# Seven groups of an MLP product on column tiles of TensorE's array

## The chip, the core and the metric

The kernel runs on one core of a Trainium2 chip. Its time is the device time of one execution in microseconds (us); the time before is the median of three runs. A profile is one further execution, taken with the hardware profiler.

## What is computed

One transformer block on a sequence of S = 2048 rows with D = 1024: layer normalization, attention of 32 heads in a sliding window of 256, a residual sum, a second layer normalization, an MLP with F = 3584 and a residual sum. Inputs and output are bfloat16. The reference, cut:

```python
x = A_x
h = x + _A_ref(_layernorm(x, axis=-1), A_wqkv, A_wo)
h2 = h + _B_ref(_layernorm(h, axis=-1), B_w1, B_w2)

def _B_ref(x, w1, w2):
    h = jnp.einsum("bsd,df->bsf", x, w1)
    h = _silu(h)
    out = jnp.einsum("bsf,fd->bsd", h, w2)
    return out
```

The change lies in the first product of the last function, `x @ w1`.

## The kernel before

The sequence is cut into NB = 4 blocks of 512 rows. The kernel first computes queries, keys, values and the attention of the blocks, with the scores of one block laid between the matmuls of the next block's projections (lines 240 and 250) by a hand-written stream; `wo_group` (line 271) multiplies by `wo`. Then comes the MLP, block by block: all of the first product of a block, then all of its second.

The first product of a block has FT = 28 column groups of 128 columns of `w1`. `h1_group(b, ft)` (line 666) computes one group: it takes one PSUM bank of [128 x 512] from a rotation of six (`next_acc`; the banks are called acc and hacc in the profile) and sums KT = 8 matmuls in it (line 669). Each of them has a [128 x 128] piece of `w1` as the stationary operand, the weights, and 512 columns of `ln2T[b]`, the transposed normalized rows, as the moving operand. TensorE loads weights with an instruction of its own (LDWEIGHTS, "PEld" in the profile) and then streams the moving operand past them. A "step" below is one of the eight values of `kt`.

```python
acc = next_acc()
for kt in range(KT):
    nc.tensor.matmul(acc, lhsT=w1[:, kt, ft * P:(ft + 1) * P], rhs=ln2T[b][:, kt, :],
                     start=(kt == 0), stop=(kt == KT - 1))
```

After each group `silu` (line 676) has ScalarE compute a tanh from the bank (line 678) and VectorE combine it with the bank into `gT` (line 679), which is the stationary operand of the second product, `mm2` (line 706). In the last block (b = 3) nothing else runs beside this loop: its 28 groups follow one another, and `mm2` follows them.

The order on every engine is the order in which the code issues instructions (`tc.manual_schedule()`); no planner moves them.

A matmul can also take a part of the array, a tile: rows of the array by columns. Its place is given by `tile_position=(row, column)`, and its output goes to the PSUM partitions of its columns. The kernel does this already in the attention's scores: `scores_xy` (matmul in line 303) and `scores_0` (line 355) run on tiles of 32 rows by 64 columns, eight of them for the four heads of a group and two halves of the keys, and `scores_c` (line 329) on tiles of 32 rows by 128 columns. Line 383 is the product of attention weights and values, on the whole array with 33 moving columns.

Of the kernel before, what the change touches and what calls it, by code (L numbers as in the profile page):

```python
# [14 lines left out]
P = 128  # L15
# [22 lines left out]
    [(0, "X", 2), (1, "Y", 1), (2, "X", 3)],  # L38
    [(1, "Y", 2), (2, "C", 1), (3, "Y", 3)],
]  # L40
SPLIT = [(0, 8), (8, 16), (16, 21), (21, 27), (27, 32)]


@with_exitstack
def kernel(
# [10 lines left out]
    nc = tc.nc  # L56
# [8 lines left out]
    KT = D // P  # L65
# [29 lines left out]
    def view(region, off, *dims):  # L95
        n = 1
        for d in dims:
            n *= d
        ap = region[:, off:off + n]
        if len(dims) == 2:  # L100
            return ap.rearrange("p (a b) -> p a b", b=dims[1])
        if len(dims) == 3:
            return ap.rearrange("p (a b c) -> p a b c", b=dims[1], c=dims[2])
        return ap
# [3 lines left out]
    w1 = view(r_w, 0, KT, F)  # L108
# [17 lines left out]
    ln2T = [view(r_a, w2_off + 4096 * 5, KT, 512), view(r_e, 0, KT, 512), view(r_e, 4096, KT, 512), view(r_e, 0, KT, 512)]  # L126
# [104 lines left out]
    def next_acc():  # L231
        acc_n[0] += 1
        return acc_banks[acc_n[0] % len(acc_banks)]
# [54 lines left out]
    def scores_xy(b, g, odd):  # L288
        q0 = odd * P
        mid, first, last = odd, odd - 2, odd + 2  # L290

        parts = [
            (mid, 0, q0, q0 + 320, 64), (mid, 1, q0 + 64, q0 + 384, 128),
            (last, 0, q0 + 256, q0 + 384, 384), (first, 1, q0, q0 + 128, 0),
            (first, 0, q0, q0 + 64, 0), (last, 1, q0 + 320, q0 + 384, 448),
        ]
        for step in range(3):
            for hh in range(4):
                for kt, half, qa, qb, col in parts[step * 2:step * 2 + 2]:
                    r0 = hh * DH  # L300
                    t = b * 4 + kt
                    k0 = (t % 4) * P + half * 64
                    nc.tensor.matmul(  # L303
                        sc[hh // 2][half * 64:half * 64 + 64, hh % 2, col:col + qb - qa],
                        lhsT=kT[t // 4][r0:r0 + DH, g, k0:k0 + 64],
                        rhs=qT[b][r0:r0 + DH, g, qa:qb],
                        start=True, stop=True, tile_position=(r0, half * 64),
                    )
        for pair in range(2):
            e = xy_ring[((b * G + g) % 2 * 2 + odd) * 2 + pair]  # L310
            tri = e[:, 0:1024].rearrange("p (h c q) -> p h c q", h=2, q=256)
            bank = sc[pair]
            both = bank[:, :, 0:192]
            both = bass.AP(tensor=both.tensor, offset=both.offset, ap=[*both.ap[:2], [320, 2], both.ap[2]])
            nc.scalar.activation(out=tri[:, :, :, 64:256], in_=both, func=ACT.Exp, scale=scale)  # L315
            nc.scalar.activation(out=e[:, 1024:1280].rearrange("p (h q) -> p h q", q=P), in_=bank[:, :, 192:320], func=ACT.Exp, scale=scale)  # L316
            four = e[:, 0:1024].rearrange("p (c q) -> p c q", q=256)
            select(four[:, :, 0:P], four[:, :, 64:64 + P], False)
            select(four[:, :, P:2 * P], four[:, :, P:2 * P], True)
# [86 lines left out]
    def attn_piece(b, g, first, last):  # L406

        for k in range(2):
            a, z = max(first - 16 * k, 0), min(last - 16 * k, 16)
            if a < z:  # L410
                attn_out(b, g + k, a, z)
                if z == 16:
                    late.append(lambda k=k: attn_transpose(b, g + k))

    class Stream:
# [3 lines left out]
        def __init__(self, b):  # L419
# [4 lines left out]
            for g in range(0, G, 2):  # L424
                if b:
                    self.bursts += [lambda g=g: scores_c(b, g)]
                    self.bursts += [lambda g=g, k=k, o=o: scores_xy(b, g + k, o) for k in range(2) for o in range(2)]
                    self.pieces += [lambda g=g, s=s: attn_piece(b, g, *s) for s in SPLIT]
                else:
# [235 lines left out]

    def h1_group(b, ft):
        acc = next_acc()
        for kt in range(KT):
            nc.tensor.matmul(acc, lhsT=w1[:, kt, ft * P:(ft + 1) * P], rhs=ln2T[b][:, kt, :],  # L669
                             start=(kt == 0), stop=(kt == KT - 1))  # L670
        return acc

    th_first = [r_e[:, 1024 * i:1024 * (i + 1)].bitcast(F32) for i in range(2)]
# [9 lines left out]
    for b in range(NB):  # L683
# [4 lines left out]
        for ft in range(FT):  # L688
            acc = h1_group(b, ft)
            run_late()  # L690
            if extra:
                extra.pop(0)[0]()
            if b == 0 and ft == 4:
                for i in (1, 2, 3, 4):
                    load_w2(i)
            silu(b, acc, ft)
            if b == 0 and 7 <= ft < 15:
                j, c = divmod(ft - 7, 2)
                wo_group(NB - 1, j, c)
# [59 lines left out]
```

## Time and profile before

| | |
|---|---|
| median of three runs | 691.17 us (691.05 to 691.21) |
| the profiled execution, first to last instruction (span) | 688.9 us (688.92) |
| the profiled execution's own time outside its span | not given by the page; the median of the runs is 2.25 us above the span |
| TensorE busy | 685.2 us (99%), 6011 matmuls and as many weight loads |
| VectorE, ScalarE, GpSimd busy | 291.2, 244.2, 160.8 us |
| granted TensorE clock, mean | 1.000 |
| one matmul of line 669 | 128x512, 379 ns from start to modelled end |
| first product of the last block | 589.3 to 637.6 us of the span |

Busy time of a matmul runs from its start to its modelled end, and matmuls overlap: the 379 ns are how long one is under way, not the distance to the next one. That distance is read from the starts. In a merged timeline row, the first number is the start of the first instruction, the second the time until the last one's end, and the xN how many instructions the row merges; a row carries the shape of its first instruction. In the view by windows, a column "0.03 (x8)" is the busy time in the window and the number of instructions that were under way in it; after TensorE's matmuls (PE) and weight loads (PEld) come the granted clock, the share of DMA and GB/s.

### The profile page before, as it was taken

How to read it: one execution, taken by the hardware profiler on the slowest of the kernel's cores; microseconds unless marked ns; L12 is line 12 of the kernel's file. 1: busy time of each engine (PE TensorE's matmuls, PEld its weight loads, DVE VectorE, ACT ScalarE, POOL GpSimd, SP SyncE). 2: the span in 40 equal slices, each digit the busy share in tenths (PEclk: the TensorE clock that was granted, in tenths of full speed). 3: DMA queues.
4: the chain of work that ended last, by engine and by line, in shares of the span. 5: the costliest groups of instructions: out<-in, count | busy, mean ns of one | idle time of the engine just before them, and what ended most of it. 6: DMA issues, size and time to landing. Idle time of an engine off the chain costs nothing.

```text
span 688.9 us, 14243 instructions
## 1 busy us (share of the span) xinstructions
PE 685.2 (99%) x6011; PEld 342.3 (50%) x6011; DVE 291.2 (42%) x613; ACT 244.2 (35%) x464; POOL 160.8 (23%) x295
## 2 busy tenths in 40 slices
PE   9999999999999999999999999999999999999998
PEld 4445555555555555544444444444444444444445
DVE  5267647744444449444316133342233251333111
ACT  7326666666667666421300033300133100233000
POOL 1006666566666656400000000000000000000000
PEclk9999999999999999999999999999999999999999
DMA  7832231126241889871023310022300123100110
GB/s 259 275 64 69 40 85 57 25 63 186 71 131 21 257 252 272 199 267 40 23 88 112 84 39 0 1 91 70 85 0 1 21 96 90 39 1 1 30 39 24
DMA packets 78641, 61.48 MB, mean 89 GB/s; under 512 B 52465, under 2 KB 62705, under 8 KB 78577
## 3 DMA queue, kind: packets, MB, share of 16 engines
q1 hardware_dynamic: 77888, 59.78, 30.2%
q8 instruction: 47, 0.77, 0.4%
q10 hardware_dynamic: 688, 0.79, 0.3%
q14 instruction: 18, 0.14, 0.1%
HBM read 39.85 MB, written 8.39 MB: 70 GB/s over the span
## 4 chain that ended last, share of the span: by engine, by line
PE 99%; DVE 0%; issue 0%
PE hacc L669 19%; PE hacc L706 18%; PE acc L250 17%; PE acc L706 11%; PE acc L669 9%; PE acc L240 7%; PE acc L271 7%; PE o_ps L383 5%; PE sc L303 3%; PE hacc L271 2%; PE sc L355 1%; PE o_ps L240 1%; PE o_ps L167 1%; PE sc L329 1%; PE acc L525 0%; PE o_ps L525 0%
## 5 line engine op out<-in xcount | busy, mean ns | idle before, releaser
L373 POOL TENSOR_SCALAR_AFFINE_SELECT r_e<-r_e 128x512 bf16<-128x512 bf16 (+1 forms) x288 | 157.8, 563 | 123.9 <-ACT r_e L363 60.8
L706 PEld LDWEIGHTS <-r_a 128*128 128x128 bf16 x952 | 90.9, 98 | 103.0
L669 PEld LDWEIGHTS <-r_w 128*128 128x128 bf16 x896 | 87.3, 98 | 104.8
L706 PE MATMUL hacc<-r_a 128*128 128x512 bf16 (+2 forms) x616 | 122.5, 360 | 0.0
L669 PE MATMUL hacc<-r_e,r_w 128*128 128x512 bf16 x456 | 100.9, 379 | 0.0
L315 ACT ACTIVATE r_e<-sc 128x768 bf16<-128x768 f32 x96 | 78.2, 814 | 47.9 <-PE sc L303 47.9
L678 ACT ACTIVATE r_n<-hacc 128x512 f32<-128x512 f32 x30 | 17.9, 597 | 178.9 <-PE hacc L669 178.9
L250 PEld LDWEIGHTS <-r_w 128*128 128x128 bf16 x512 | 47.1, 98 | 55.0 <-issue 1.0
L706 PE MATMUL acc<-r_a 128*128 128x512 bf16 x336 | 74.0, 379 | 0.0
L252 DVE CAST r_a<-acc 128x512 bf16<-128x512 f32 x56 | 38.7, 692 | 57.7 <-PE acc L250 57.4
L250 PE MATMUL acc<-r_t,r_w 128*128 128x512 bf16 x256 | 59.6, 380 | 0.0
L250 PE MATMUL acc<-r_w 128*128 128x512 bf16 x256 | 57.8, 380 | 0.0
L383 PEld LDWEIGHTS <-r_e 128*128 128x128 bf16 x1440 | 47.4, 96 | 17.9
L669 PE MATMUL acc<-r_e,r_w 128*128 128x512 bf16 x216 | 49.1, 379 | 0.0
L271 PE MATMUL acc<-r_o,r_a 128*128 128x512 bf16 x208 | 48.7, 380 | 0.0
L383 PE MATMUL o_ps<-r_a,r_e 128*128 128x33 bf16 x1440 | 48.1, 178 | 0.0
L721 DVE SCALAR_TENSOR_TENSOR r_t<-hacc,r_t 128x512 bf16<-128x512 f32 (+2 forms) x22 | 14.0, 635 | 56.7 <-PE hacc L706 56.7
L316 ACT ACTIVATE r_e<-sc 128x256 bf16<-128x256 f32 x96 | 37.6, 392 | 0.0
L271 PEld LDWEIGHTS <-r_a 128*128 128x128 bf16 x256 | 23.4, 98 | 26.9
L721 DVE SCALAR_TENSOR_TENSOR r_t<-acc,r_t 128x512 bf16<-128x512 f32 x12 | 8.3, 692 | 64.2 <-PE acc L706 64.2
L679 DVE SCALAR_TENSOR_TENSOR r_a<-r_n,hacc 128x512 bf16<-128x512 f32 x30 | 20.6, 687 | 33.0 <-ACT r_n L678 33.0
L669 PE MATMUL hacc<-r_a,r_w 128*128 128x512 bf16 x144 | 33.0, 379 | 0.0
(100 smaller groups left out, 539.6 us busy)
## 6 DMA issues: line engine op xcount, KB each, us to landing
r_w<-in_B_w_dram SPq DMA_DIRECT2D x8, 896.0 KB, 5.2
r_a<-in_B_w_dram SPq DMA_DIRECT2D x7, 1024.0 KB, 7.5
r_w<-in_A_wqkv_dram SPq DMA_DIRECT2D x4, 1024.0 KB, 7.8
h_dram<-r_t SPq DMA_DIRECT2D x16, 256.0 KB, 3.1
r_t<-h_dram SPq DMA_DIRECT2D x16, 256.0 KB, 2.8
out_dram<-r_t SPq DMA_DIRECT2D x31, 128.0 KB, 1.7
r_o<-in_A_x_dram SPq DMA_DIRECT2D x15, 256.0 KB, 4.6
r_e<-h_dram SPq DMA_DIRECT2D x3, 1024.0 KB, 5.7
```

Source lines behind the costliest of these rows:

```text
L240: nc.tensor.matmul(acc, lhsT=lnT_b[b % 2][:, kt, j * P:(j + 1) * P], rhs=wv[:, kt, c * 512:(c + 1) * 512], start=(kt == 0), stop=(kt == KT ...
L250: nc.tensor.matmul(acc, lhsT=wqk[:, kt, col0:col0 + P], rhs=lnT_b[b % 2][:, kt, :], start=(kt == 0), stop=(kt == KT - 1))
L252: copy(out=(qT, kT)[which][b][:, g, :], in_=acc)
L271: nc.tensor.matmul(acc, lhsT=qT[b][:, g, j * P:(j + 1) * P], rhs=wo[:, g, c * 512:(c + 1) * 512], start=(g == 0), stop=(g == G - 1))
L303: nc.tensor.matmul(sc[hh // 2][half * 64:half * 64 + 64, hh % 2, col:col + qb - qa], lhsT=kT[t // 4][r0:r0 + DH, g, k0:k0 + 64], rhs=qT[b] ...
L315: nc.scalar.activation(out=tri[:, :, :, 64:256], in_=both, func=ACT.Exp, scale=scale)
L316: nc.scalar.activation(out=e[:, 1024:1280].rearrange("p (h q) -> p h q", q=P), in_=bank[:, :, 192:320], func=ACT.Exp, scale=scale)
L373: nc.gpsimd.affine_select(out=dst, in_=src, pattern=[[0, n] for n in dst.shape[1:-1]] + [[sgn, P]], compare_op=ALU.is_ge if upper else ALU ...
L383: nc.tensor.matmul(o_ps[pair][:, qt * 2 + hh, 0:VW], lhsT=chunk_of(i, bank, piece, pair, hh), rhs=v[:, b * 4 + kt, g * 4 + pair * 2 + hh, ...
L669: nc.tensor.matmul(acc, lhsT=w1[:, kt, ft * P:(ft + 1) * P], rhs=ln2T[b][:, kt, :], start=(kt == 0), stop=(kt == KT - 1))
L706: nc.tensor.matmul(acc[:, 0:c1 - c0], lhsT=gT[:, ft, j * P:(j + 1) * P], rhs=w2[ft // 4][:, ft % 4, c0:c1], start=(ft == 0), stop=(ft == F ...
L721: nc.vector.scalar_tensor_tensor(out=t_out[j % 2][:, c0:c1], in0=acc[:, 0:c1 - c0], scalar=0.5, in1=t_in[j % 2][:, c0:c1], op0=ALU.mult, o ...
```

## The change

A table names seven groups of the last block and the width of their column tiles, 64 or 32. For these, every matmul of a step is replaced by two or four, each over all 128 rows of the array and 64 or 32 of its columns, with that part of the weights and the whole moving operand of 512 columns; each writes its own part of the bank's partitions. The tiles of one step come one after another in the code, before the next step. All other groups are as before.

```diff
     [(0, "X", 2), (1, "Y", 1), (2, "X", 3)],
     [(1, "Y", 2), (2, "C", 1), (3, "Y", 3)],
 ]
+COLS = {(3, 8): 64, (3, 9): 64, (3, 12): 32, (3, 13): 32, (3, 16): 64, (3, 17): 32, (3, 20): 32}
 SPLIT = [(0, 8), (8, 16), (16, 21), (21, 27), (27, 32)]
...
     def h1_group(b, ft):
         acc = next_acc()
+        m = COLS.get((b, ft), P)
         for kt in range(KT):
-            nc.tensor.matmul(acc, lhsT=w1[:, kt, ft * P:(ft + 1) * P], rhs=ln2T[b][:, kt, :],
-                             start=(kt == 0), stop=(kt == KT - 1))
+            for c in range(0, P, m):
+                tiled = {} if m == P else {"tile_position": (0, c)}
+                nc.tensor.matmul(acc[c:c + m, :], lhsT=w1[:, kt, ft * P + c:ft * P + c + m], rhs=ln2T[b][:, kt, :],
+                                 start=(kt == 0), stop=(kt == KT - 1), **tiled)
         return acc
```

## The prediction

> **What bounds the kernel now.** I began with the page: its first two parts say which engine has no time to spare.
>
> ```profile
> span 688.9 us, 14243 instructions
> PE 685.2 (99%) x6011; PEld 342.3 (50%) x6011; DVE 291.2 (42%) x613; ACT 244.2 (35%) x464; POOL 160.8 (23%) x295
> ...
> PEclk9999999999999999999999999999999999999999
> ...
> PE 99%; DVE 0%; issue 0%
> ```
>
> TensorE (PE) works in 99% of the span, at full granted clock, and the chain that ended last is PE alone. A nanosecond that the change adds to PE's stream is added to the end, and nothing else can be gained. Next, the same chain in order of time, cut to the stage of the change:
>
> ```profile
> 598.07 6.91 PE hacc L669 x32
> 604.98 3.45 PE acc L669 x16
> 608.43 6.91 PE hacc L669 x32
> 615.34 3.45 PE acc L669 x16
> 618.79 6.91 PE hacc L669 x32
> ```
>
> 6.91 us for 32 matmuls is 216 ns a matmul: 512 columns, one after another, with no gap. A group is 8 of these, 1.73 us. Groups 8 to 20 run from 603.1 to 625.5 us, and the seven in question hold 56 matmuls, 12.1 us. PE waits for nobody in this stage (its list of waits between 589 and 640 us is empty); ScalarE waits 1.13 us in each group for PE.
>
> The third reading is of the one thing in this kernel that resembles the change: the score matmuls of the attention, which already run on tiles of 32 rows by 64 columns. The timeline of PE around the first of them:
>
> ```profile
> 48.29 0.59 PE L250 MATMUL acc<-r_w 128*128 128x512 bf16 x2
> 48.81 0.42 PE L355 MATMUL sc<-r_a 32*64 32x320 bf16 x16
> 49.17 0.39 PE L240 MATMUL acc<-r_w,r_t 128*128 128x512 bf16 x1
> ```
>
> In ns the starts are 48503 (the second full matmul), 48812 (first tiled one) and 49169 (first full one after). Each of the eight tiles gets two matmuls, 320+192 or 384+128 columns: 512 for each tile, as much as one step of the change. The burst took 357 ns. Were the 16 matmuls (4096 columns) to run one by one, they would need 1.7 us, and were only the two column halves in turn, some 430 ns. So two 64-column tiles over the same rows do stream at once. The other view is the number of matmuls and weight loads in flight in slices of the burst at 110.01 us (line 303):
>
> ```profile
> 110.01:110.04 0.03, 0.03 (x8) 0.03 (x8) 1.00 0.00 0
> 110.04:110.17 0.13, 0.13 (x8) 0.13 (x16) 1.00 0.00 0
> ...
> 110.20:110.23 0.03, 0.03 (x16) 0.03 (x8) 1.00 0.00 0
> ```
>
> In the second slice (PE first, then PEld) the count of loads goes from 8 to 16 while the same 8 matmuls still stream: the next weights of every tile are loaded behind its present matmul.
>
> **The change part by part.** Seven groups, 56 full matmuls with their 56 loads, go away; 3 groups x 8 steps x 2 and 4 x 8 x 4 make 48 + 128 = 176 tiled pairs, 120 matmuls and 120 loads more. Nothing else moves: the order and the waits on the other four engines are those of before, no DMA is added, and only the first matmul of a group waits, as before, for the reader of its PSUM bank.
>
> Streaming. If all tiles of a step stream together, a step is still 512 columns, 216 ns, and 56 steps cost what they cost now. For two tiles the burst above shows it; for four column tiles there is no row. The nearest is the 32x128 burst (line 329), four row tiles of 128 columns: its steps start at 0, 66, 122 and 178 ns, so after the first they are 56 ns apart, as with full 128-column matmuls. The small delay between tiles (3 ns each) does not add up from step to step. Taken: 0.
>
> Weight loads. In the score bursts each tile starts its second matmul 24 ns late (160 ns after its first, where 320 columns need 136), and no later step does: that is the first load, which nothing hides. After it the loads lie behind 213 ns of streaming. Here that cover must hold a load of every tile in each step. If it is gone, each step pays those 24 ns: 56 x 24 = 1.3 us more.
>
> The Trainium skill, "TensorE: Matmul & The Clock Gate", Part 3 (the mechanism), has a rule against this change: a weight load overlaps running matmuls only if its row group differs, and here all tiles use all rows. By that rule every step would show its load, and the sum would be +2.4 us or more. The slices above show loads for the row groups that are streaming, so I go by the row.
>
> Changing the array's shape. From a full 512-column matmul to the first tiled one: 48812 - 48503 = 309 ns, where 216 would do: +93. The four direct changes of this kind in the trace are all 309. Back: a full matmul starts 120 ns after the last tiled one of 64 columns (27 ns): +93 again. The first full one holds up its successor by 10 ns (226 for 216). So a run of neighbouring tiled groups pays 93 + 24 + 93 + 10 = 220 ns, and 3 ns for each further tile: 223 with two, about 230 with four. The burst at 48.81 agrees: (309 - 216) + (357 - 216) + 10 = 244, of which some 24 are its own eight tiles and second matmul.
>
> There are four runs: groups 8-9 (64 wide), 12-13 (32), 16-17 (64, then 32), 20 (32). 223 + 230 + 230 + 230 = 913 ns. Inside the third the shape changes from 64 to 32. No row shows such a change. Its bounds are 0 (it is treated as another tile) and 93 + 24 = 117 (it is a change like the others); I take 117, since both kinds of change that the trace has cost the same 93. The skill's "TensorEngine Tiling (Array Packing)", Tiling Modes, says that a change of mode drains the array and a change of tile does not, which would give 117 too.
>
> Issue. A 32-wide group issues 64 instructions in 1.73 us, one in 27 ns. In the attention (line 383) load and matmul pairs start 25 ns apart, one instruction in 12.5 ns, so this fits. Taken: 0.
>
> Behind PE. A group's result comes at most some 20 ns later; ScalarE and VectorE, with over 1 us to spare per group and six PSUM banks in rotation, don't hold PE up.
>
> Sum: 913 + 117 = 1030 ns. On the profiled execution's own span, 688.92 + 1.03 = 689.95 us. The page gives no time for that execution beyond its span; the median of the runs is 691.17, 2.25 above the span, which I keep: 692.20 us. What a measurement of this kernel can tell from no change, 0.2%, is 1.38 us, so the bound lies at 692.55, and the forecast is just inside.
>
> **The rivals.**
>
> *A, the forecast: only the changes of shape cost.* From 0.89 us (four times 223, nothing inside the third run) to 1.5 us: the 1.1 above (with some tens of ns for the four-tile first load), plus 3 ns per further tile in every step, 24 x 3 + 32 x 9 = 0.36. Its own range is 692.05 to 692.7.
>
> *B, the steps are held up a little.* A load of 128 rows in a shape of which the trace has only 32 rows, or four loads in place of two, is not quite hidden: 24 ns x 56 = 1.3 us, 2.4 in all: 693.5, and with twice that 694.9. For it: no row has tiles of 128 rows, nor steps of accumulation on tiles. Against it: the third step of the 303 burst starts 56 ns after the second with 128 columns of cover; here there are 512.
>
> *C, on the slower side: the four 32-column tiles don't all stream at once.* Each of them reads the same 128 rows of the moving operand in its own stream; the trace has two streams over the same rows, never four. If the four go two by two, 32 steps x 216 = 6.9 us, 7.9 in all: 699.1. It decides from 11 ns a step on (0.35 us over 32 steps); the 64-wide groups would still be as forecast.
>
> *D, column tiles of 128 rows run one after another:* 24 x 216 + 32 x 648 = 25.9 us, 718.1. Against it stands the burst at 48.81, in which two halves over the same 32 rows ran together.
>
> *E, not slower:* the changes of shape cost nothing, because what drains in the score bursts is particular to 32-row tiles: 691.2. A real gain has no source: the only part of a step that isn't streaming is 2.5 ns, 0.14 us over 56 steps.
>
> **How the numbers follow.** A has 0.47 (of which 0.09 beyond 692.55), B 0.24, C 0.12, D 0.09, E 0.05, and a gain for which I have no mechanism 0.03. Within 0.2%: 0.38 + 0.05 = 0.43. Slower: 0.09 + 0.24 + 0.12 + 0.09 = 0.54. Faster: 0.03. The likeliest single case lies inside the bound by 0.35 us, yet everything unknown lies on the slow side of it. The range takes in A, B and C (0.83): 691.9 to 699.4.
>
> **What would show it.** In the profile after, the group line of the first MLP product has forms 128*64 (48) and 128*32 (128), all of 512 columns. By A, the first tiled matmul of groups 8-9 starts 309 ns after the full one ahead of it, and the first full one after them 16 x 216 + 24 + 3 + 93 = 3576 ns later; groups 12 and 13 the same with four starts within 10 ns of each other, eight steps 216 ns apart; the span is 689.9 to 690.3. A step of 240 ns says B; 430 ns in the 32-wide groups alone says C; starts of two tiles 216 ns apart say D; no pause at either end says E. It is wrong if the pause differs from 93 ns in this shape, above all between 64 and 32, or if time appears outside these groups.

## The result, and the profile after

| | before | after |
|---|---|---|
| median of 20 runs each | 691.16 us | 692.20 us |
| ratio, 95% interval | | 1.0014 (1.0007 to 1.0020) |
| span of the profiled execution | 688.92 us | 691.5 us (its own time 693.19) |
| first product of the last block, first to last matmul's start | 48.13 us | 49.14 us |

The change makes the kernel 1.04 us slower, 0.14%: inside the 0.2% that the prediction named as the bound. The intervals of the later runs reach 0.1 to 0.25% (0.6 to 1.6 us) to either side, so effects of 1 us and less are read from the starts of the matmuls in the traces, which repeat to about 10 ns from run to run in this part of the kernel.

The spans of the two profiled executions differ by 2.6 us, more than the medians, and that has to be cleared first. The page and the list of PE's waits of the changed kernel:

```profile
span 691.5 us, 14483 instructions
PE 686.1 (99%) x6131; PEld 341.9 (49%) x6131; DVE 291.3 (42%) x613; ACT 244.1 (35%) x464; POOL 160.8 (23%) x295
...
PE 98%; DMA 2%; ACT 0%; ACTq 0%; issue 0%; DVE 0%
```

```profile
PE o_ps L168 <- DVE eps L148: 1.1, 1, 1.1
PE acc L251 <- DMA r_w<-r_o: 0.8, 1, 0.8
PE acc L241 <- ACT r_w L220: 0.3, 1, 0.3
PE acc L241 <- DMA r_w<-in_A_wqkv_dram: 0.3, 1, 0.3
PE tp L219 <- DVE r_e L467: 0.2, 1, 0.2
```

The chain (the work that ended last, followed back step by step) has a DMA share that is new, and all the waits below the first line stand in the first 23 us: in this execution a transfer of the first weights (`in_A_wqkv`) and one of the first transposed rows (`r_w<-r_o`) came later. The four waits that the kernel before did not have make 1.6 us. From the first matmul to the MLP the two traces need 282.51 and 284.07 us, 1.56 us apart, with the same instructions there. The nine kernels below whose code ahead of the MLP is also unchanged needed 282.78 to 284.06. So this is scatter of the start, not the change. Between the MLP's start and the end only the stage of the change differs: 112.32, 96.69, 96.69, then 48.13 against 49.14, then 48.65 us (first products and what follows them, by the starts of the matmuls). (Lines have moved by 4 in the MLP: 673 is 669.)

The chain that ended last, cut to the same stretch as before, shows where the 1.0 us went:

```profile
599.62 7.03 PE hacc L673 x40
606.65 3.56 PE acc L673 x24
610.21 7.13 PE hacc L673 x80
617.34 3.57 PE acc L673 x24
620.91 7.24 PE hacc L673 x80
628.15 3.56 PE acc L673 x16
```

The pieces are four and two groups, 6.91 and 3.45 us long before. The excesses are 0.12, 0.11, 0.22, 0.12, 0.33 and 0.11 us: about 0.1 us at each place where full groups and tiled groups meet, or the width changes. The numbers of matmuls in a piece (40 in place of 32, 80 in place of 32) do not show in the times.

The pause itself stands in the starts around groups 8-9, of matmuls and of weight loads; the rows are from narrow windows of the timeline:

```profile
604.42 0.38 PE L673 MATMUL hacc<-r_e,r_w 128*128 128x512 bf16 x1
604.73 0.41 PE L673 MATMUL hacc<-r_e,r_w 128*64 128x512 bf16 x2
608.00 0.38 PE L673 MATMUL acc<-r_e,r_w 128*64 128x512 bf16 x2
608.31 0.39 PE L673 MATMUL acc<-r_e,r_w 128*128 128x512 bf16 x1
```

```profile
604.21 0.10 PEld L673 LDWEIGHTS <-r_w 128*128 128x128 bf16 x1
604.73 0.11 PEld L673 LDWEIGHTS <-r_w 128*64 128x64 bf16 x2 [0.42 <-issue]
```

It is 309 ns from the last full matmul to the first tile and 312 from the last tile to the next full one, where steps of one shape are 216 apart. Among full matmuls a load starts 2 ns behind the matmul ahead of its own, 214 ns early. At the change the first load starts 307 ns behind the last full matmul and only 2 ns ahead of its own. So the pause is not a load that takes longer: in it neither a load nor a matmul of the new shape starts. What the array waits for, the trace does not show.

### The profile page after: what moved, and what is told of

It reads as the page before. It is cut to its first block, busy times and chain, and to the rows that moved or that the text cites. A ratio compares the mean times of both kernels' runs of the same rounds, so it can differ in the third digit from the quotient of the medians.

```text
span 691.5 us, 14483 instructions
## 1 busy us (share of the span) xinstructions
PE 686.1 (99%) x6131; PEld 341.9 (49%) x6131; DVE 291.3 (42%) x613; ACT 244.1 (35%) x464; POOL 160.8 (23%) x295
## 4 chain that ended last, share of the span: by engine, by line
PE 98%; DMA 2%; ACT 0%; ACTq 0%; issue 0%; DVE 0%
PE hacc L673 19%; PE hacc L710 18%; PE acc L251 17%; PE acc L710 10%; PE acc L673 9%; PE acc L272 7%; PE acc L241 7%; PE o_ps L384 5%; PE sc L304 3%; PE hacc L272 1%; DMA r_w<-in_A_wqkv_dram 1%; PE sc L356 1%; DMA r_w<-r_o 1%; PE sc L330 1%; PE o_ps L241 0%; PE acc L526 0%
## 5 line engine op out<-in xcount | busy, mean ns | idle before, releaser
L673 PEld LDWEIGHTS <-r_w 128*128 128x128 bf16 (+2 forms) x1016 | 87.2, 98 | 106.2 <-issue 4.3
L673 PE MATMUL hacc<-r_e,r_w 128*128 128x512 bf16 (+2 forms) x560 | 101.4, 379 | 0.0
L251 PEld LDWEIGHTS <-r_w 128*128 128x128 bf16 x512 | 47.1, 98 | 56.0 <-issue 2.3
L673 PE MATMUL acc<-r_e,r_w 128*128 128x512 bf16 (+1 forms) x232 | 49.3, 379 | 0.0
```

The lines of the kernel that those rows point to most:

```text
L251: nc.tensor.matmul(acc, lhsT=wqk[:, kt, col0:col0 + P], rhs=lnT_b[b % 2][:, kt, :], start=(kt == 0), stop=(kt == KT - 1))
L673: nc.tensor.matmul(acc[c:c + m, :], lhsT=w1[:, kt, ft * P + c:ft * P + c + m], rhs=ln2T[b][:, kt, :], start=(kt == 0), stop=(kt == KT - 1) ...
```

## The experiments

The theory, A: a change of the array's shape costs, a tiled group in itself does not. Its rivals: G, each tiled group costs 0.143 us; I, each added pair of load and matmul costs 8.4 ns. All three give 1.0 us for the seven groups of the change.

**All 28 groups of the last block, 64 wide, then 32 wide**

```diff
-COLS = {(3, 8): 64, (3, 9): 64, (3, 12): 32, (3, 13): 32, (3, 16): 64, (3, 17): 32, (3, 20): 32}
+COLS = {(3, ft): 64 for ft in range(28)}
```

(and with 32 in the second kernel)

> All 28 groups of the last block's first product on 64-column tiles: one run of neighbouring tiled groups, one change of shape in and one out. A (only changes of shape cost, as in the changed kernel: entry 93, first load 24, second tile 3, exit 93, first full one after 10): +0.22 us over the kernel before, steps 216 ns apart. G (each tiled group costs the 0.143 us that 1.00 us over seven groups gives): 28 x 0.143 = +4.0 us. I (each added matmul and load costs, 1.00 us / 120 = 8.4 ns): 224 x 8.4 = +1.9 us.

> The same with 32-column tiles in all 28 groups. A: +0.22 us (first load 11 in place of 24, three further tiles 10 in place of 3), the first tiles of two steps 216 ns apart over 224 steps. G: +4.0 us. I: 672 x 8.4 = +5.6 us.

Measured: 691.91 and 691.69 us against 691.10, ratios 1.0009 (1.0000 to 1.0018) and 1.0008 (0.9999 to 1.0016). That is at most 1.2 us, too little for G and I. In the traces the 28 groups, with the pauses at both ends, take 0.23 and 0.22 us more than before. The chain of the 32-wide kernel:

```profile
599.73 6.91 PE hacc L673 x128
606.63 3.45 PE acc L673 x64
610.09 6.91 PE hacc L673 x128
617.00 3.45 PE acc L673 x64
```

Four times as many matmuls as before stand in the same 6.91 us. So four 32-column tiles over all 128 rows stream at once, and their loads stay hidden, over 224 steps.

**The same seven widths side by side**

```diff
-COLS = {(3, 8): 64, (3, 9): 64, (3, 12): 32, (3, 13): 32, (3, 16): 64, (3, 17): 32, (3, 20): 32}
+COLS = {(3, 8): 64, (3, 9): 64, (3, 10): 64, (3, 11): 32, (3, 12): 32, (3, 13): 32, (3, 14): 32}
```

> As many groups of each width as the change has (three of 64, four of 32), but side by side as groups 8 to 14: one run with one change of width inside in place of four runs with one. A: 0.226 + 0.104 (64 to 32: 93 and a first load of 11) = +0.33 us over the kernel before, 0.67 less than the changed kernel. G and I: +1.0 us, as the changed kernel.

Measured: 691.46 us, ratio 1.0003 (0.9994 to 1.0012). The stage is 48.47 us, 0.34 over the kernel before, where the change costs 1.01. The tiles are the same in number and width; only three of the four ways in and out are gone.

**Every second group tiled**

```diff
+COLS = {(3, ft): 64 for ft in range(0, 28, 2)}
```

> Every second of the 28 groups on 64-column tiles: 14 runs of one group. A: 14 x 0.226 = +3.2 us. G: 14 x 0.143 = +2.0 us. I: 112 x 8.4 = +0.9 us.

Measured: 694.26 us against 691.10, ratio 1.0042 (1.0029 to 1.0055). In the trace 3.17 us, from the entry to the end of the stage, where A had 3.2; the median's interval alone (2.0 to 3.8 us) would not exclude G's 2.0. Half as many tiled groups as in the first kernel cost fourteen times as much.

**64 and 32 in turn**

```diff
+COLS = {(3, ft): (64, 32)[ft % 2] for ft in range(28)}
```

> All 28 groups tiled, in turn 64 and 32 wide: one run with 27 changes of width inside, 14 from 64 to 32 and 13 from 32 to 64. A (each is a change of shape like the others): 0.22 + 14 x 0.104 + 13 x 0.117 = +3.2 us. Rival W (only a change to narrower tiles stops the array, one to wider ones costs nothing): 0.22 + 14 x 0.104 = +1.7 us. G: 28 x 0.143 = +4.0 us.

Measured: 694.53 us against 691.53, ratio 1.0049 (1.0036 to 1.0062); in the trace 3.39 us. The last tile of one width and the first of the other start 309 ns apart in both directions, +93, so W falls: a change to wider tiles stops the array as well. The chain:

```profile
595.24 3.69 PE acc L673 x48
598.93 7.38 PE hacc L673 x96
606.30 3.69 PE acc L673 x48
```

3.69 us for two groups in place of 3.45. A pair has two changes: 93 + 11 + 3 ns into 32 (pause, first load, the start of the second 64-wide tile behind the first) and 93 + 24 + 10 into 64 (10 for the fourth 32-wide tile behind the first), 234 ns together. A's 3.2 had left out the distance between a step's tiles, which each change pays again.

**Same columns, other rows**

In the kernel before, the query and key groups of blocks 2 and 3 were put on 64-column tiles:

```diff
+            if b >= 2:
+                for c in (0, 64):
+                    nc.tensor.matmul(acc[c:c + 64, :], lhsT=wqk[:, kt, col0 + c:col0 + c + 64], rhs=lnT_b[b % 2][:, kt, :],
+                                     start=(kt == 0), stop=(kt == KT - 1), tile_position=(0, c))
+                continue
```

> The kernel before with its query and key groups of blocks 2 and 3 (line 250) on two 64-column tiles of 128 rows, so that 22 score bursts on 32x64 tiles are followed by a matmul of the same column width and other rows. Changes of shape of any kind go from 152 to 182. A (any change of shape stops the array): the matmul after a burst starts 120 ns after the last tiled one of 64 columns, as before; 30 x 93 + 28 x 14 (first loads of 24 for 10) = about +3.2 us. Rival C (only a change of column width stops it): that gap falls to about 30 ns, and the sum is 8 x 93 + 28 x 14 = about +1.1 us.

Measured: 695.37 us against 691.53, ratio 1.0054 (1.0041 to 1.0068): +3.8 us (2.8 to 4.7). From the first matmul of line 303 (308 here) to the MLP the trace has 180.22 against 176.63 us, +3.59; A's sum had 3.2, and the 0.4 beyond it is not taken apart here. One of the bursts, with the matmul behind it:

```profile
125.60 0.43 PE L308 MATMUL sc<-r_a 32*64 32x320 bf16 x24
125.96 0.41 PE L252 MATMUL acc<-r_w 128*64 128x512 bf16 x2
```

From the burst's start it is 0.36 us to that matmul, as to a full one in the kernel before (110.02 to 110.38). In all 22 places the first 128x64 matmul starts 117 or 118 ns after the last 32x64 one. The expectation's rival C is out: rows count as columns do. The pause is not tied to 32-row tiles (the prediction's case E) either: it stands between any two of the shapes 128x128, 128x64, 128x32 and 32x64 that meet here.

**The order of the tiles**

What lets the tiles stream together? The next kernel has the seven groups of the change with its loops swapped:

```diff
-        for kt in range(KT):
-            for c in range(0, P, m):
+        for c in range(0, P, m):
+            for kt in range(KT):
```

> The seven groups of the change, with the two loops swapped: all eight steps of one tile are issued before the next tile's first. F (matmuls start in the order of the program, so tiles stream together only where they stand next to each other): 3 x 8 x 216 + 4 x 24 x 216 = 25.9 us more than the changed kernel, +26.9 over the kernel before. T (each tile works off its own queue, whatever the order): as the changed kernel, +1.0 us.

Measured: 703.99 us against 691.53, ratio 1.0180 (1.0167 to 1.0194). Both expectations fail: the stage is 11.5 us longer than in the changed kernel, neither 0 nor 25.9. The chain at groups 8 and 9, in the banks hacc and acc, says how:

```profile
606.79 0.03 PE acc L673
606.83 0.19 PE hacc L673
607.01 0.03 PE acc L673
607.04 0.19 PE hacc L673
```

Here group 9's first tile (acc) and group 8's second tile (hacc) run by turns, although in the program all of group 8 stands ahead. The profile does not name a matmul's columns; which tile a start belongs to is read from the 216 ns between a tile's steps. In ns, the first tile of group 8 starts its steps at 0, 240, 456, 672, 888 and on; the second tile starts at 893, with the fifth step of the first. So matmuls do not start strictly in program order: at 893 three of the first tile (steps 6 to 8) still wait and are passed.

I first took it for a reach of four among all waiting matmuls (V), and ran chunks of four and of two steps a tile:

```diff
+        for c, kt in ((c, kt) for k0 in range(0, KT, 4) for c in range(0, P, m) for kt in range(k0, k0 + 4)):
```

> The seven groups of the change, issued in chunks: four steps of one tile, four of the next, and so on, then the other four steps of each. V (the run with whole tiles one after another showed a second tile's first matmul starting with the first tile's fifth, so among the waiting matmuls the first four can be taken; played through by hand with 216 ns a step): the 64-wide runs as in the changed kernel, with both tiles starting together; groups 12-13 695 ns more, group 17 and group 20 671 ns more each: +2.0 us over the changed kernel, +3.0 over the kernel before. With a reach of three: +5.3 over the changed kernel, 240 ns of it in groups 8-9; with five: +1.4. F (program order alone): +17.7 over the changed kernel.

> The same in chunks of two steps. V (reach of four): nothing more than the changed kernel, +1.0 us over the kernel before, all four tiles under way from the first step on or soon after. With a reach of three or two: +0.7 to 0.8 over the changed kernel, all in the 32-wide groups. F (program order alone): +8.3 over the changed kernel.

Measured: 692.37 and 692.34 us against 691.15, ratios 1.0018 (1.0008 to 1.0027) and 1.0016 (1.0006 to 1.0026). In the stage 0.16 and 0.04 us over the changed kernel. Chunks of two agree with V; chunks of four refute it, which wanted 2.0 there. In groups 12-13 of that kernel the four tiles start at 0, 14, 27 and 40 ns; the fourth has passed nine waiting matmuls, three of each other tile.

The theory that is left, Q: matmuls are handed out in program order, each tile holds up to three waiting ones, and only a full tile stops the handing out. It was made from the three orders above, so it needed one that it had not seen: six steps of each tile, then two.

```diff
+        for c, kt in ((c, kt) for ks in (range(0, 6), range(6, 8)) for c in range(0, P, m) for kt in ks):
```

> The seven groups in chunks of six steps of one tile, six of the next, then two of each. Q (matmuls are handed out in program order, each tile has its own queue that holds three waiting ones, and only a full queue stops the handing out; this gives 11.4, 0.1 and 0.03 us over the changed kernel for chunks of eight, four and two, where 11.5, 0.16 and 0.03 were measured in the stage): the second tile starts with the third step of the first, 459 ns after it; +5.3 us over the changed kernel, +6.3 over the kernel before. With queues of two: 675 ns, +8.6; of four: 243 ns, +2.5, both over the changed kernel. F (program order alone): the second tile starts after six steps, 1320 ns.

Measured: 697.65 us against 691.33, ratio 1.0089 (1.0066 to 1.0113). The second tile starts at 461 ns (Q: 459), and the stage is 54.56 us, 5.42 over the changed kernel (Q: 5.3). Queues of two or four would have given 8.6 or 2.5 us. Q holds in its numbers. Whether three matmuls or the loads between them are what fills a tile, these runs do not tell, as every matmul came with a load.

No version here beats the kernel before. The traces show no source for a gain either: a tiled step takes the 216 ns of a full one, and the pauses come on top.

## Why the prediction was right, point by point

- **The bound.** PE sets the end, and the median grew by what the stage grew: 1.01 us in the stage, 1.04 in the median. That the median met the forecast of 692.20 to the digit is luck: by its interval the change costs 0.5 to 1.4 us. What was foreseen is the stage's 1.01 against 1.03.
- **Streaming at 216 ns a step**, taken from the 32x64 burst for two tiles and, without a row of its own, for four: right. The first tiled matmul of groups 8-9 starts 309 ns after the full one, and the first full one after them 3577 ns later; the prediction had 309 and 3576. The tiles of a 32-wide step start within 9 to 10 ns, and their first starts are 216 ns apart.
- **Hidden loads.** Right, against the rule that the prediction quoted from the Trainium skill ("TensorE: Matmul & The Clock Gate", Part 3). All tiles use the same rows here, and yet 224 steps of four loads each stay at 216 ns (0.22 us in all, both ends included); here the measurement decides. The kernel before showed as much already: its full matmuls use all rows too, and start 216 ns apart with a new load each. (The same section of the page also allows a load ahead into a background weight buffer, which the prediction did not weigh.)
- **93 ns for each change of shape.** Right on the way in (309 or 310 ns in place of 216, four times) and between 64 and 32 (309 ns), where no row existed and the upper bound was taken. On the way out the next full matmul starts 311 or 312 ns after the last tile's start, 96 over a step, 3 ns more than the price from the score bursts. That the change between two tiled shapes pays agrees with what the skill's "TensorEngine Tiling (Array Packing)", Tiling Modes, says of changes of mode.
- **The mis-sized term** is the first load of a 32-wide run. I took the 64-wide tile's 24 ns for all; a 32-wide tile's second step comes 11 ns late (227 for 216). That this delay is the load is the prediction's reading; no run isolates it. The runs cost 226, 219, 340 and 220 ns where the sum had 223, 230, 347 and 230: 1.005 us in place of 1.030.
- **The chances.** The point was right, the spread was not well placed: B, C and D had 0.45 together because the trace had no tiles of 128 rows and no four tiles over the same rows. The 32x64 bursts, with two halves over the same rows at once, spoke against D, and their third step, on time behind 128 columns, against B; on C they were silent. The runs of 28 groups leave nothing of the three.
- **The span** predicted for the profile (689.9 to 690.3) was missed at 691.5, by the late first weights and rows of that execution. A forecast of one execution's span cannot be surer than the scatter of its start, 1.5 us here.

## What to carry to other kernels

Splitting a full matmul of 512 columns into column tiles was free here with the tiles alternating in the program (28 groups: 0.22 us, all of it at the ends); it gained nothing, as the full steps left no gap. Fewer columns were not tried. What cost was each change of the array's shape, rows or columns, about 0.1 us with the first load, 0.22 us for there and back. So count the changes, not the tiled matmuls, and put tiled work of one shape side by side. When tiles are to run together, issue them in turn: two or four steps of one tile in a row cost 0.2 us or less here, six cost 5.4 and eight 11.5.

## What was not expected of the hardware

Matmuls on different tiles started out of program order. All five orders run here fit a tile with one matmul streaming and three waiting, where the handing out goes on to other tiles until a fourth would have to wait: in the 64-wide groups the second tile started after 4 steps of 8 (893 ns) and after 2 of 6 (461 ns), and at once in chunks of 4 (13 ns) and of 2 (8 ns).
